# Decode block with backward pass: which arena slot a backward buffer gets, and where dependent side steps are cut

## The chip, the cores and the metric

The kernel runs on one core of one Trainium2 chip. The metric is device time in microseconds. A time is the median of several executions of the whole program; the profile is one further execution of it with the hardware profiler on.

## The reference

The kernel computes one decode step of a transformer block and all gradients of it. `A_` is attention over a cache, `B_` is a gated feed-forward layer:

```
x: 4 rows of 512;  k_cache, v_cache: 4 x 32 heads x 4096 x 128 (bf16)
q  = layernorm(x) @ wq                      # 32 heads of 128
p  = softmax(q k^T / sqrt(128));  o = p v
h  = x + o @ wo
h2 = h + (silu(ln(h) @ w1) * (ln(h) @ w3)) @ w2
out_0 = h2; out_1..out_8 = gradients of x, k_cache, v_cache, wq, wo, w1, w3, w2 for grad_out
```

The 128 pairs of batch and head have one query row each. The gradient of V for one head is the outer product of p and dO, the gradient of K the outer product of dS and q, with dS = p * (dO v^T - c) * scale. Both are as large as the caches, 1 MB a head, so the caches are read (V twice) and two arrays of the same size are written: 282 MB written and 423 MB read.

## The kernel before

**The arena.** Nearly all large buffers live in one tile, `arena`, of 23 slots of 4160 bf16 values in each partition, a little over 1 MB a slot. `Slot(name)` takes a slot and `give()` returns it; the order of the instructions is the order in which the code emits them, on each engine, and a slot may be given back as soon as its last use has been emitted: whoever takes it next waits by semaphore for that use to be over. `free` is a queue, so the slot given back first is taken first. `Slot2` takes two neighbouring slots for a buffer of 2 MB.

**Forward part.** For each of 128 heads, K and V are loaded, K is transposed, scores and softmax are computed for two heads at a time, and K scaled by p and V are multiplied to a small matrix. This part and the layer between (`mid`) are the same in both kernels.

**Backward part, single heads.** The first `SP` = 32 heads are worked one by one (steps `s`). In a step, V of head s + 5 is transposed on PE and evacuated by ACT (`front`, `V_T`, L790 and L791), `more_V` forms the V gradient 9 heads ahead of `s` (`grad_V`), `grad_K(s)` forms the K gradient; DVE writes each outer product into a slot (L796), and SP stores it (L807, L1234). From step 20 on (`part["B"]`), heads in preparation for the pairs below and side buffers share the arena: `part["pairs"]` names the 16 slots 0 to 5 and 8 to 17, eight pairs; the side buffers (`SIDE`) take the first slot of `free` that is not among them. Slot 7 holds small rows for the whole part.

**Backward part, pairs.** The other 96 heads go in 48 pairs (steps `t`). `load_pair` (L1259) loads V of two heads into a `Slot2`, `front_pair` transposes it (L1276 on PE, L1277 on ACT) three pairs ahead, `more_V` and `grad_pair` form the V gradient four pairs ahead and then the K gradient of pair t, both on DVE at L1357, stored by SP at L1367. POOL prepares the p column of each pair (L1354) and the dO window (L1268). `replicate_pair` writes replicated rows of q or dO (L1344 on PE, L1347 on ACT).

**Side work.** Everything else of the backward part, the gradients of x and of the weights, is in `side_work`, a generator. Each pair step runs two of its units before and two after its own gradients, a unit being what stands between two `yield`s. It computes dq (L1006 to L1011), puts it into the row buffer `flat` (POOL loads, L1015), transposes wq and forms dx (L1026 to L1047), stores dx (L1048), forms four pieces of the wq gradient in slots `gwq` (matmul L974, evacuation L968, store L1057), then loads w2 (L528), takes the row buffers `rows1` and `rows2`, loads grad_out into the first (`gr_bf`, L1066, on POOL), writes transposed rows into both (L1074 on PE, L1076 on ACT), forms the feed-forward output (`o_ps` on PE at L1086, the sum on DVE at L1091, stored at L1092) and the gradients of w2 (L1101), w1 and w3 (L1117) and wo (L1128).

Around `rows1` the code before reads:

```python
                nc.sync.dma_start(out=out_4[cc * P:(cc + 1) * P, :], in_=st.b(HD))
                st.give()
            flat.give()
            fs.give()
            w2 = load_w2()

            r1, r2 = Slot("rows1"), Slot("rows2")
```

At that moment `flat` and `fs` occupy slots 18 and 6, and the last `gwq` store is that of slot 22. The queue gives `w2` the slots 19 and 21, then `rows1` slot 22 and `rows2` slot 18.

Of the kernel before, what the change touches and what calls it, by code (L numbers as in the profile page):

```python
# [18 lines left out]
NSLOT = 23  # L19
JQ = 8  # L20
NPE = 1
SP = 32
NPAIR = 8


@with_exitstack
def kernel(
# [25 lines left out]
    B = A_x.shape[0]  # L53
# [9 lines left out]
    DC = D // P  # L63
# [43 lines left out]

    free = deque(range(NSLOT))
    part = {"B": False, "side_done": False}
    SIDE = ("Pp", "wq2", "dqflat", "fin", "rows1", "rows2", "oflat", "w2a", "w2b", "gwq", "gw2", "gw13", "gwo")  # L110
    arena = slotp.tile([P, NSLOT * SLOT], BF16, name="arena")

    class Slot:
        def __init__(self, name, src=free):
            if name in SIDE and part["B"]:
                self.i = next(i for i in free if i not in part["pairs"])
                free.remove(self.i)
            else:
                self.i = src.popleft()
            self.t = arena[:, self.i * SLOT:(self.i + 1) * SLOT]  # L120

        def b(self, n=4096):
# [6 lines left out]
            return self.t[:, 0:SJ * Dh].rearrange("p (j d) -> p j d", d=Dh)  # L129

        def give(self):
            free.append(self.i)

    class Slot2:
        @staticmethod
        def choices():
            at = {i: n for n, i in enumerate(free)}
            return [(max(at[i], at[i + 1]), i) for i in (range(0, NSLOT - 1, 2) if part["side_done"] else sorted(part["pairs"])[::2])
                    if i in at and i + 1 in at]

        def __init__(self):
            self.i = min(self.choices())[1]
# [2 lines left out]
            self.t = arena[:, self.i * SLOT:(self.i + 2) * SLOT]  # L145

        def give(self):
            free.append(self.i)
            free.append(self.i + 1)


    rows_t = pers.tile([32 + B, D], FP32, name="rows_t")
# [45 lines left out]
    for i in range(2):  # L198
        t = fcon.tile([P, 64], BF16, name=f"onesw{i}")
# [316 lines left out]
    def two_slots(nm):  # L516
        return [Slot(nm + "a"), Slot(nm + "b")]
# [7 lines left out]
    def load_w2():  # L525
        sl = two_slots("w2")
        for i in range(2):
            nc.sync.dma_start(out=sl[i].b(7 * D).rearrange("p (c j) -> p c j", c=7),  # L528
                              in_=B_w2.rearrange("(p c) j -> p c j", c=FC)[:, i * 7:(i + 1) * 7, :])
        return sl  # L530
# [247 lines left out]
    REP = B  # L778
    reps = {}
    V2s, VTs = {}, {}  # L780
# [34 lines left out]
    NV2 = 7  # L815
    vring = deque()
    nv = {"next": 0}
# [137 lines left out]
    with ExitStack() as c2:  # L955
# [44 lines left out]
        def side_work():  # L1000
# [4 lines left out]
            t = rs.f(2080)[:, 1536:1536 + NH]  # L1005
            nc.vector.tensor_tensor(out=t, in0=c_rep[:], in1=kPT[:], op=ALU.mult)  # L1006
            nc.vector.tensor_tensor(out=t, in0=dq_ps[:, 0:NH], in1=t, op=ALU.subtract)
            nc.vector.tensor_scalar(out=dqT_bf[:], in0=t, scalar1=scale, scalar2=None, op0=ALU.mult)
            pt = psg.tile([P, P], BF16, tag="gps", name="pt_dq")
            nc.tensor.transpose(pt[:], dqT_bf[:], ident_b[:])  # L1010
            nc.scalar.copy(out=dqr_bf[:], in_=pt[:])  # L1011
            flat = Slot("dqflat")
            yield
# [6 lines left out]
            for cc in range(DC):  # L1020
                wq2 = wq2s.popleft()
# [14 lines left out]
                load_wq2(cc + 2)  # L1036
                yield
            yield
            fs = Slot("fin")
            dxhat, lnbx, xh = (fs.f(3 * D)[0:B, k * D:(k + 1) * D] for k in range(3))  # L1040
            xhat_bf = fs.t[0:B, 6 * D:7 * D]
# [3 lines left out]
            layernorm_bwd_rows(lnbx, dxhat, xh, rstd_x[:], B)  # L1045
            dx_bf = rs.t[0:B, 3328:3328 + D]
            nc.vector.tensor_tensor(out=dx_bf, in0=dh, in1=lnbx, op=ALU.add)  # L1047
            nc.gpsimd.dma_start(out=o1_2, in_=dx_bf)  # L1048
            yield
            for cc in range(DC):  # L1050
                st = Slot("gwq")
                for n8 in range(HD // 512):
                    grad_unit(st.b(HD)[:, n8 * 512:(n8 + 1) * 512], xhat_bf[0:B, cc * P:(cc + 1) * P],
                              flat.b(HD)[0:B, n8 * 512:(n8 + 1) * 512])
                    yield
                grad_flush()
                nc.sync.dma_start(out=out_4[cc * P:(cc + 1) * P, :], in_=st.b(HD))  # L1057
                st.give()
            flat.give()
            fs.give()  # L1060
            w2 = load_w2()

            r1, r2 = Slot("rows1"), Slot("rows2")
            hh_rows, dg_rows, du_rows = r1.t[0:B, 0:F], r1.t[0:B, F:2 * F], r2.t[0:B, 0:F]
# [22 lines left out]
            for sl in w2:  # L1087
                sl.give()
            yield
            h2_bf = rs.t[0:B, 3328:3328 + D]  # L1090
            nc.vector.tensor_tensor(out=h2_bf, in0=hrows, in1=o2_ps[0:B, :], op=ALU.add)  # L1091
            nc.gpsimd.dma_start(out=o0_2, in_=h2_bf)  # L1092
            yield
            for i in range(2):
                st = Slot("gw2")
                hw = hh_rows[:, i * 7 * P:(i + 1) * 7 * P].rearrange("b (p k) -> b k p", k=7)
# [7 lines left out]
            oflat = Slot("oflat")  # L1104
# [49 lines left out]
        def replicate(nm_, i0):  # L1154
            if i0 >= NH or (nm_, i0 // REP) in reps:
                return
            K_ = 8 * B if i0 < 8 * B else P
            rows = dOrows_bf if nm_ == "rdo" else qrows_bf
            ps = psrep.tile([P, REP, Dh], FP32, tag="rep", name="rep_ps")
            for i in range(REP):  # L1160
                nc.tensor.matmul(ps[:, i, :], lhsT=ident_b[0:K_, i0 + i:i0 + i + 1].to_broadcast([K_, P]), rhs=rows[0:K_, :],
                                 start=True, stop=True)
            rt = rep_bufs[nm_][i0 // REP % 2]
            nc.scalar.copy(out=rt, in_=ps[:])
            reps[nm_, i0 // REP] = rt
# [28 lines left out]
        def front(s):  # L1194
            hl = s % B
            if s not in VTs:
                for g in range(SJ // GW):
                    V_T(s, psT, range(g, g + 1))
                    if hl == 0 and g == 0:
                        rows_out()  # L1200
                    if hl == 0 and g == 2:
                        rows_T()
            VT = VTs[s].heads()
            if hl == 0:
                rows["acc"] = psD.tile([P, 512], FP32, tag="dP", name="dP_ps")
            dO_window(s + 2)
            for u in range(2):
                for c in range(4):
                    j0 = 8 * c + 4 * u
                    nc.tensor.matmul(rows["acc"][32 * c:32 * (c + 1), :], lhsT=zq_window(zd[hl], 2 * hl + u),  # L1210
                                     rhs=VT[:, j0:j0 + 4, :], start=(hl == 0 and u == 0),
                                     stop=(hl == B - 1 and u == 1), tile_position=(0, 32 * c))
            if hl == B - 1:
                rows["ps"] = rows.pop("acc")
            sl = VTs.pop(s)
            (vring if nv["next"] < SP and len(V2s) + len(VTs) + len(vring) < NV2 else free).append(sl.i)

        def group_dS(g):
            i0 = g * B
# [22 lines left out]
        NT = (NH - SP) // 2  # L1242
        H0 = SP // B
        pV, pP2, pdS, psl = {}, {}, {}, {}
        npv = {"next": 0}
# [13 lines left out]
            nc.sync.dma_start(out=pV[t].t[:, 0:2 * SJ * Dh], in_=two_heads(A_v_cache, t))  # L1259

        def load_pairs(t):
            while npv["next"] < NT and (npv["next"] <= t or len(V2s) + 2 * len(pV) < 6 and len(Slot2.choices()) > 1):
                load_pair()

        def dO_pair(t):
# [44 lines left out]
        Pp, zt, P2b = {}, [], []  # L1310
# [23 lines left out]
        def replicate_pair(nm_, q):  # L1334
            if q >= NT // B or (nm_, "p", q) in reps:
                return
            s = SP + q * 2 * B
            K_ = 8 * B if s + 2 * B <= 8 * B else P
            rws = dOrows_bf if nm_ == "rdo" else qrows_bf
            ps = psrep.tile([P, REP, Dh], FP32, tag="rep", name="rep_ps")  # L1340
            for i in range(REP):
                for a in range(2):
                    n = s + i + a * B
                    nc.tensor.matmul(ps[64 * a:64 * (a + 1), i, :], lhsT=ident_b[0:K_, n:n + 1].to_broadcast([K_, P // 2]),  # L1344
                                     rhs=rws[0:K_, :], start=True, stop=True, tile_position=(0, 64 * a))
            rt = rep_bufs[nm_][(H0 + q) % 2]
            nc.scalar.copy(out=rt, in_=ps[:])  # L1347
            reps[nm_, "p", q] = rt
# [24 lines left out]
        def more_V(upto):  # L1373
            while gvd["n"] < min(SP, upto):
                s = gvd["n"]
                P_pairs(s)
                replicate("rdo", s - s % REP)
                grad_V(s)
                P_pairs(s + 1)
                P_pairs(s + 2)  # L1380
                gvd["n"] += 1
                if s % REP == 2 and s + 2 < SP:
                    replicate("rdo", s + 2)
                if s >= SP - 2:
                    P2_pair(s - SP + 2)
            while gvd["t"] < NT and SP + 2 * gvd["t"] + 2 <= upto:
                t = gvd["t"]
                P2_pair(t)
                replicate_pair("rdo", t // B)
                grad_pair(out_3, t, pP2.pop(t), reps["rdo", "p", t // B][:, t % B, :])  # L1390
                P2_pair(t + 1)
                gvd["t"] += 1
                if t % B == 2:
                    replicate_pair("rdo", t // B + 1)
# [57 lines left out]
        for t in range(NT):  # L1452
            s = SP + 2 * t
# [46 lines left out]
```

## Time and profile before

| | |
|---|---|
| median of 3 runs | 1698.37 us (1697.37 to 1699.48) |
| profiled execution | 1698.35 us, of which its span 1696.6 us |
| busy, share of the span | PE 73%, DVE 73%, ACT 57%, POOL 19% |
| DMA | 707.45 MB, mean 417 GB/s over the span |
| span in parts | forward and middle to about 740 us, single heads to about 960 us, pairs to the end |

A busy share is an average over the whole span; the slices of the page (40 of 42.4 us each) and the stretches of the trace show where it is high. A queue wait is read in three parts: the engine and line that waited, what ended the wait, and the sum, number and longest of the waits. "DMA out_dram<-arena" as the end of a wait means that a store had to land before its slot could be written again. The time from issue to landing of a DMA contains the time that it stood in the queue behind others.

### The profile page before, as it was taken

Reading aid. Unit: us, or ns where it says so; the run is one execution under the profiler, and the core shown is the slowest. Engines: PE = TensorE matmul, PEld = TensorE weight load, DVE = VectorE, ACT = ScalarE, POOL = GpSimd, SP = SyncE. Lnnn points to the kernel's source line nnn. Section 1 sums busy time; section 2 is a strip of 40 time slices with the busy share of each in tenths; the row PEclk is TensorE's granted clock in tenths of the full one; section 3 lists DMA queues with packets and bytes.
Section 4 is the critical chain, followed back from the end, with each engine's and each line's share of the span. In section 5 each row is a group of like instructions: output and inputs, shape, how many; then the busy total and the mean of one; then the engine's idle time right before and its main releaser. Section 6 shows DMA issues by size and latency. Waiting matters only on the chain. (4 is left out here: it accounts for less than half of the span.)

```text
span 1696.6 us, 37845 instructions
## 1 busy us (share of the span) xinstructions
PE 1245.9 (73%) x16228; PEld 953.4 (56%) x16228; DVE 1234.4 (73%) x1198; ACT 959.0 (57%) x1490; POOL 329.5 (19%) x583
## 2 busy tenths in 40 slices
PE   5889888888888888878877655666727767677552
PEld 4777766676677676756565544544425445445431
DVE  5989999999999987667764676575636665565582
ACT  3555444454455444677666566666628766566551
POOL 1211223222222222222331111021004110100000
PEclk9999999999999999798898689867659776666675
DMA  9999999999999999999999999999997999999998
GB/s 400 424 425 423 424 423 425 424 424 424 416 422 413 424 402 400 391 411 425 426 426 426 416 427 429 430 429 429 430 423 309 418 425 426 429 428 430 429 429 343
DMA packets 81000, 707.45 MB, mean 417 GB/s; under 512 B 8748, under 2 KB 12984, under 8 KB 15296
## 3 DMA queue, kind: packets, MB, share of 16 engines
q1 hardware_dynamic: 80416, 704.94, 99.0%
q8 instruction: 127, 2.08, 0.5%
q14 instruction: 41, 0.34, 0.0%
q0 software_dynamic: 416, 0.10, 0.0%
HBM read 422.59 MB, written 282.34 MB: 416 GB/s over the span
## 5 line engine op out<-in xcount | busy, mean ns | idle before, releaser
L1277 ACT COPY arena<-pt_tps 128x1024 bf16<-128x1024 bf16 x384 | 369.5, 1024 | 208.4 <-PE pt_tps L1276 208.0
L1276 PE MATMUL pt_tps<-ident_b,arena 128*128 128x128 bf16 x3072 | 309.7, 273 | 205.5 <-DMA arena<-in_A_v_cache_dram 124.1
L1276 PEld LDWEIGHTS <-arena 128*128 128x128 bf16 x3072 | 266.1, 126 | 307.2 <-issue 154.9
L1357 DVE TENSOR_TENSOR arena<-arena 128x8192 bf16<-128x8192 bf16 x48 | 212.3, 4424 | 255.6 <-DMA out_dram<-arena 223.7
L462 PE MATMUL M_ps<-arena 128*128 128x130 bf16 x4096 | 286.5, 222 | 37.8 <-DMA arena<-in_A_v_cache_dram 37.2
L447 DVE TENSOR_TENSOR arena<-arena 128x4096 bf16<-128x4096 bf16 x128 | 292.5, 2285 | 24.8 <-POOL arena L443 24.8
L462 PEld LDWEIGHTS <-arena 128*128 128x128 bf16 x4096 | 253.6, 99 | 58.7 <-DMA arena<-in_A_v_cache_dram 51.7
L354 DVE STREAM_TRANSPOSE arena<-arena 128x512 f32<-128x512 f32 (+1 forms) x321 | 250.6, 797 | 0.0
L349 ACT COPY arena<-pt_tps 128x1024 bf16<-128x1024 bf16 x128 | 129.4, 1012 | 186.7 <-PE pt_tps L348 151.7
L1357 DVE TENSOR_TENSOR arena<-dS,arena 128x8192 bf16<-128x8192 bf16 x48 | 212.4, 4427 | 19.6 <-DMA out_dram<-arena 19.4
L791 ACT COPY arena<-pt_tps 128x1024 bf16<-128x1024 bf16 x128 | 121.9, 1026 | 28.4 <-PE pt_tps L790 25.9
L360 POOL TENSOR_TENSOR W<-qrep,wmask 128x128 bf16<-128x128 bf16 x128 | 120.7, 943 | 85.4 <-PE S_ps L380 70.5
L1354 POOL COPY arena<-arena 128x128 bf16<-128x128 bf16 x48 | 38.8, 808 | 501.9 <-ACT arena L1331 276.3
L443 POOL COPY arena<-P_all 128x64 bf16<-128x64 bf16 x128 | 32.4, 253 | 413.6 <-ACT P_all L437 410.6
L790 PE MATMUL pt_tps<-ident_b,arena 128*128 128x128 bf16 x1024 | 82.1, 236 | 25.5 <-ACT arena L791 25.5
L1291 PE MATMUL dP_ps<-arena 128*32 128x512 bf16 x768 | 86.0, 484 | 7.8 <-ACT arena L1277 7.6
L790 PEld LDWEIGHTS <-arena 128*128 128x128 bf16 x1024 | 70.8, 108 | 36.1 <-issue 34.9
L437 ACT COPY P_all<-pt_P 32x64 bf16<-32x64 bf16 x256 | 51.9, 203 | 55.1 <-PE pt_P L433 52.9
L796 DVE TENSOR_TENSOR arena<-P,arena 128x4096 bf16<-128x4096 bf16 x29 | 66.3, 2296 | 20.1 <-DMA out_dram<-arena 19.7
L348 PE MATMUL pt_tps<-ident_b,arena 128*128 128x128 bf16 x1024 | 80.5, 223 | 0.0
L472 PE MATMUL kP_ps<-arena,onesw 128*32 128x512 bf16 x1024 | 79.2, 386 | 0.0
L796 DVE TENSOR_TENSOR arena<-dS,arena 128x4096 bf16<-128x4096 bf16 x32 | 73.5, 2302 | 6.6 <-DMA out_dram<-arena 6.2
(245 smaller groups left out, 1595.4 us busy)
## 6 DMA issues: line engine op xcount, KB each, us to landing
out_dram<-arena SPq DMA_DIRECT2D x96, 2048.0 KB, 27.7
arena<-in_A_v_cache_dram SPq DMA_DIRECT2D x160, 1024.0 KB, 15.8
arena<-in_A_k_cache_dram SPq DMA_DIRECT2D x128, 1024.0 KB, 15.4
arena<-in_A_v_cache_dram SPq DMA_DIRECT2D x48, 2048.0 KB, 31.7
out_dram<-arena SPq DMA_DIRECT2D x72, 1024.0 KB, 19.7
arena<-in_A_wq_dram SPq DMA_DIRECT2D x8, 1024.0 KB, 16.1
arena<-in_B_w_dram SPq DMA_DIRECT2D x8, 896.0 KB, 15.1
out_dram<-arena SPq DMA_DIRECT2D x6, 896.0 KB, 28.6
```

The lines of the kernel that those rows point to most:

```text
L349: nc.scalar.copy(out=KT[:, c * GW:(c + 1) * GW, :], in_=pt[:])
L354: nc.vector.transpose(out=KT[:, c * w_:(c + n) * w_], in_=Kn[:, c * w_:(c + n) * w_])
L360: nc.gpsimd.tensor_tensor(out=W[:, hl], in0=qrep[:, :, s:s + 1].to_broadcast([P, 4, 32]), in1=wmask[:, hl, None, :].to_broadcast([P, 4, 32 ...
L447: nc.vector.tensor_tensor(out=PK[:, :, 0:Dh].rearrange("p j (r t) -> p j r t", t=2), in0=Ks[s].heads().rearrange("p j (r t) -> p j r t", t=2),
L462: nc.tensor.matmul(hold["M"][:], lhsT=Vn[:, j, :], rhs=PK[:, j, :], start=(j == 0), stop=(j == SJ - 1))
L790: nc.tensor.transpose(pt[:, i, :], v[:, g * GW + i, :], ident_b[:])
L791: nc.scalar.copy(out=v[:, g * GW:(g + 1) * GW, :], in_=pt[:])
L796: nc.vector.tensor_tensor(out=dst.rearrange("p j (r t) -> p j r t", t=2), in0=col2[:, :, None, :].to_broadcast([P, SJ, Dh // 2, 2]), in1=r ...
L1276: nc.tensor.transpose(pt[:, i, :], v[:, g * GW + i, :], ident_b[:])
L1277: nc.scalar.copy(out=v[:, g * GW:(g + 1) * GW, :], in_=pt[:])
L1291: nc.tensor.matmul(rows["acc"][32 * c:32 * (c + 1), :], lhsT=zt[t % B][:, 32 - m:64 - m], rhs=v[:, j0:j0 + 4, :], start=(pl == 0 and u == ...
L1357: nc.vector.tensor_tensor(out=dst.rearrange("p (j r t) -> p j r t", r=Dh // 2, t=2), in0=col2[:, :, None, :].to_broadcast([P, 2 * SJ, Dh / ...
```

## The change

The change has four parts, all in the backward part.

1. Slots are chosen by an age, the number of slots stored since the slot was given back. A V slot that was only read is entered with an age of 4 more. From step 20 on a slot outside the pairs is taken by a side buffer, and by a gradient too if its age is at least `OLD` = 9; otherwise the oldest of all is taken. A `Slot2` is the pair whose younger half is oldest, whether it held a V pair or a gradient pair. `lnb`, a scratch buffer of dx, joins the side buffers.
2. `load_pairs` loads ahead only if the pair that it would take has an age of at least `OLD` - 2.
3. `flat` and `fs` are given back before the slot of the last `gwq` store, not after it.
4. Nine `yield`s are added to `side_work` and two removed, between steps that depend on each other, and `replicate_pair("rdo", 0)` is issued when the last single group has used its third head.

The diff, with the parts that only rename left out:

```diff
+OLD = 9
...
+    given = {"n": 0}
+
+    def age(i):
+        return given["n"] - given.get(i, -NSLOT)
+
+    def gave(*slots, stored=True):
+        given["n"] += len(slots) if stored else 0
+        for i in slots:
+            given[i] = given["n"] - (0 if stored else 4)
+            free.append(i)
...
-            if name in SIDE and part["B"]:
-                self.i = next(i for i in free if i not in part["pairs"])
-                free.remove(self.i)
-            else:
-                self.i = src.popleft()
+            self.i = src[0]
+            if part["B"] and src is free:
+                lone = sorted((i for i in free if i not in part["pairs"]), key=age, reverse=True)
+                self.i = lone[0] if name in SIDE or lone and age(lone[0]) >= OLD else max(free, key=age)
+            src.remove(self.i)
...
-            at = {i: n for n, i in enumerate(free)}
-            return [(max(at[i], at[i + 1]), i) for i in (range(0, NSLOT - 1, 2) if part["side_done"] else sorted(part["pairs"])[::2])
-                    if i in at and i + 1 in at]
+            return [(-min(age(i), age(i + 1)), i) for i in (range(0, NSLOT - 1, 2) if part["side_done"] else sorted(part["pairs"])[::2])
+                    if i in free and i + 1 in free]
...
             nc.vector.tensor_scalar(out=dqT_bf[:], in0=t, scalar1=scale, scalar2=None, op0=ALU.mult)
+            yield
+            yield
             pt = psg.tile([P, P], BF16, tag="gps", name="pt_dq")
             nc.tensor.transpose(pt[:], dqT_bf[:], ident_b[:])
+            yield
             nc.scalar.copy(out=dqr_bf[:], in_=pt[:])
...
             yield
+            yield
             fs = Slot("fin")
...
             nc.vector.tensor_tensor(out=dx_bf, in0=dh, in1=lnbx, op=ALU.add)
+            yield
+            yield
             nc.gpsimd.dma_start(out=o1_2, in_=dx_bf)
-            yield
...
                 nc.sync.dma_start(out=out_4[cc * P:(cc + 1) * P, :], in_=st.b(HD))
+                if cc == DC - 1:
+                    flat.give()
+                    fs.give()
                 st.give()
-            flat.give()
-            fs.give()
             w2 = load_w2()
+            yield
...
             for sl in w2:
                 sl.give()
             yield
+            yield
             h2_bf = rs.t[0:B, 3328:3328 + D]
             nc.vector.tensor_tensor(out=h2_bf, in0=hrows, in1=o2_ps[0:B, :], op=ALU.add)
+            yield
             nc.gpsimd.dma_start(out=o0_2, in_=h2_bf)
-            yield
...
-            (vring if nv["next"] < SP and len(V2s) + len(VTs) + len(vring) < NV2 else free).append(sl.i)
+            if nv["next"] < SP and len(V2s) + len(VTs) + len(vring) < NV2:
+                vring.append(sl.i)
+            else:
+                gave(sl.i, stored=False)
...
-            while npv["next"] < NT and (npv["next"] <= t or len(V2s) + 2 * len(pV) < 6 and len(Slot2.choices()) > 1):
+            while npv["next"] < NT and (npv["next"] <= t or len(V2s) + 2 * len(pV) < 6 and len(Slot2.choices()) > 1
+                                          and -min(Slot2.choices())[0] >= OLD - 2):
                 load_pair()
...
                 if s % REP == 2 and s + 2 < SP:
                     replicate("rdo", s + 2)
+                elif s % REP == 2:
+                    replicate_pair("rdo", 0)
```

More of the change, by code (lines that the diff above doesn't have):

```diff
@@ L109 @@
     part = {"B": False, "side_done": False}
-    SIDE = ("Pp", "wq2", "dqflat", "fin", "rows1", "rows2", "oflat", "w2a", "w2b", "gwq", "gw2", "gw13", "gwo")
+    SIDE = ("Pp", "lnb", "wq2", "dqflat", "fin", "rows1", "rows2", "oflat", "w2a", "w2b", "gwq", "gw2", "gw13", "gwo")
     arena = slotp.tile([P, NSLOT * SLOT], BF16, name="arena")
+    given = {"n": 0}
[6 more added lines that the diff above has]
+            free.append(i)
     class Slot:
         def __init__(self, name, src=free):
-            if name in SIDE and part["B"]:
-                self.i = next(i for i in free if i not in part["pairs"])
-                free.remove(self.i)
-            else:
-                self.i = src.popleft()
+            self.i = src[0]
[3 more added lines that the diff above has]
+            src.remove(self.i)
             self.t = arena[:, self.i * SLOT:(self.i + 1) * SLOT]
@@ L131, in give @@
         def give(self):
-            free.append(self.i)
+            gave(self.i)
     class Slot2:
@@ L147, in give @@
         def give(self):
-            free.append(self.i)
-            free.append(self.i + 1)
+            gave(self.i, self.i + 1)
     rows_t = pers.tile([32 + B, D], FP32, name="rows_t")
```

## The prediction

> **What bounds the kernel now.** I read three views in this order. First the page's slices: DMA is the resource that is full, all the way, except in two places.
>
> ```profile
> DMA  9999999999999999999999999999997999999998
> GB/s 400 424 425 423 424 423 425 424 424 424 416 422 413 424 402 400 391 411 425 426 426 426 416 427 429 430 429 429 430 423 309 418 425 426 429 428 430 429 429 343
> ...
> out_dram<-arena SPq DMA_DIRECT2D x96, 2048.0 KB, 27.7
> ...
> arena<-in_A_v_cache_dram SPq DMA_DIRECT2D x48, 2048.0 KB, 31.7
> ```
>
> No engine passes 73% busy. 707 MB at 430 GB/s would take 1645 us; the span is 1696.6 us. So the time is bytes over rate, and only a stretch in which the DMA queue runs dry can be won back. The slice with 309 GB/s (1272 to 1315 us) is such a stretch. The last slice is the drain of the last stores and stays. The two landing times say how deep the queue is: a store lands 27.7 us after its issue, and 27.7 us at 430 GB/s is 11.9 MB. An engine may therefore be late by almost that much before the queue is empty.
>
> Second, busy time and rate in stretches around the dip, and one earlier stretch (columns: stretch, PE, PEld, DVE, ACT and POOL busy, clock, DMA share, GB/s):
>
> ```profile
> 928.00:946.00 18.00, 12.13 (x128) 9.88 (x124) 16.67 (x12) 9.55 (x12) 3.94 (x3) 0.81 0.99 395
> 946.00:1190.00 244.00, 156.02 (x1635) 117.13 (x1636) 155.27 (x88) 152.12 (x180) 39.83 (x37) 0.78 1.01 429
> 1190.00:1250.00 60.00, 36.85 (x297) 25.10 (x297) 38.56 (x19) 31.49 (x41) 1.50 (x5) 0.59 1.01 430
> 1250.00:1262.00 12.00, 0.00 (x0) 0.00 (x0) 0.00 (x0) 0.00 (x0) 0.00 (x0) 0.50 1.00 425
> 1262.00:1276.00 14.00, 6.19 (x69) 4.11 (x69) 6.93 (x2) 6.98 (x9) 1.61 (x5) 0.62 0.92 389
> 1276.00:1300.00 24.00, 18.73 (x206) 12.15 (x203) 9.09 (x9) 18.58 (x23) 5.01 (x3) 0.93 0.62 253
> 1300.00:1320.00 20.00, 14.50 (x155) 10.46 (x153) 19.61 (x10) 17.59 (x23) 13.21 (x7) 0.84 1.01 390
> 1320.00:1440.00 120.00, 83.09 (x726) 56.17 (x724) 72.28 (x36) 80.54 (x106) 12.11 (x20) 0.70 1.01 425
> ```
>
> From 1250 to 1262 no engine executes anything, and the DMA lives on its backlog; the bill comes later. Third, who waited for whom between 1220 and 1320 us (total, times, longest):
>
> ```profile
> POOL arena L1066 <- DMA out_dram<-arena: 55.2, 1, 55.2
> ...
> PE pt_tps L1276 <- ACT arena L1277: 35.2, 16, 28.0
> ACT arena L1076 <- DMA out_dram<-arena: 28.9, 1, 28.9
> DVE arena L1357 <- POOL arena L1354: 19.9, 2, 19.6
> POOL arena L1354 <- ACT arena L1331: 18.4, 1, 18.4
> DVE arena L1091 <- PE o_ps L1086: 14.5, 1, 14.5
> ```
>
> One cause, in four steps. `rows1` takes slot 22, whose last wq-gradient store (L1057) was issued at 1238.07 us and lands 28.5 us later, with only the two w2 loads (1.8 MB) issued between that store and the reuse. The load of `gr_bf` (L1066) blocks POOL and the copy of `pt_Tr` (L1076) blocks ACT until 1267. Behind ACT stand the V evacuations (L1277), so PE stands still for 28.0 us; behind POOL stand the P pairs (L1354), so DVE waits 19.6 us. When PE comes back, `o_ps` is late and DVE, in order, waits 14.5 us at L1091 with the outer products behind it.
>
> **What the Trainium skill says.** "DMA: Bandwidth & Descriptors", section "Where 436 GB/s comes from", gives 435 GB/s as the ceiling of the 16 ports; the steady 429 to 430 agree, so there is no faster rate to hope for. The same page, "Anatomy of one DMA", says that DMA engines do not wait on semaphores, the issuing sequencer does. The trace agrees: at 1250 to 1262 everything issued goes on at 425 GB/s while every engine is blocked. "Perfetto Trace Analysis", "Optimization Strategy", says to find the gaps on the most-contended resource within its regime and follow the semaphore that ends them; the three views do this.
>
> **The change part by part.** I followed both allocators, and the order in which each program's DMAs are issued, and for each reuse of a slot counted the megabytes issued after the store that it must see landed. A reuse with more than about 12 MB behind its store waits for nothing; one with less waits for the difference, but leaves that much in the queue when it is released.
>
> (1) *Row buffers.* `flat` and `fs` are given back before the last gradient's slot, and side buffers take the unpaired slot that is longest without a store. `rows1` and `rows2` get slots 6 and 21 (those of `flat` and `fs`) instead of 22 and 18. These were read by PE alone: no store stands before L1066 or L1076. The four waits above go. Worth, against 430 GB/s: 14 x (1 - 389/430) = 1.3, 24 x (1 - 253/430) = 9.9, 20 x (1 - 390/430) = 1.9, together **13.1 us**. What is late next: the w2 loads, gw2 and gw13 slots now have 13 MB or more behind their stores; the outer products keep 10.5 to 11.5 MB as before, which costs DVE some 4.7 us of idle time a pair step (223.7 us over 48) and the DMA nothing.
>
> (2) *Slots by age and pairs like stored ones.* At the change from single heads to pairs, DVE waited in the window 895 to 946 us:
>
> ```profile
> DVE arena L1357 <- DMA out_dram<-arena: 15.5, 2, 14.2
> ...
> DVE arena L1357 <- ACT arena L1347: 11.9, 1, 11.9
> ```
>
> The 14.2 us is an outer product in slots 2 and 3, whose store had 5.2 MB behind it; in the new order that product goes into slots 14 and 15, with 11.5 MB behind. The lowest value left for DVE is 8.4, as before. The loss here is 18 x (1 - 395/430) = 1.5 us. Gain between 0 and 1.5; I take 1.0, as it is two waits out of three. Against it: the first V pair is loaded one step later (12.6 MB ahead of its use instead of 14.7), and one wq load on SP now waits for a store with 6.3 MB behind it. Behind that load stand a V pair and the stores; SP is released with 6.3/0.43 = 14.7 us of queue left, so I take 0, bounds 0 and 2 us.
>
> (3) *`replicate_pair("rdo", 0)` earlier*: the same instructions, 8 matmuls and one ACT copy of 0.58 us, moved ahead of the V transposes. This takes the 11.9 us wait above; it is inside the 1.5 us already counted, so 0 more.
>
> (4) *Separate units.* Net 7 more yields, at 4 units a pair step 1.75 steps of about 14.7 us (6.3 MB at 430 GB/s) later for all side work, its SP stores and loads and its four POOL row loads included. The last side store moves from pair step 40 to 41 of 48; six steps follow, so the end is the same. Waits such as PE on `dqT_bf` (8.6 us) and DVE at L1091 go, but under a full queue: 0 on their own. Bound: 0.5 us gain for an emptier neighbourhood, 1 us loss for a moved side store at the drain.
>
> (5) The stretch 1320 to 1440 runs at 425: 120 x (1 - 425/430) = 1.4 us. The part that is the queue refilling would go, the part that belongs to the side stores would stay; I take 0.3.
>
> Sum: 13.1 + 1.0 + 0.3 = 14.4 us off the profiled execution's 1698.35 us (span 1696.6 and 1.75 around it), which is the median of 1698.37 as good as exactly: **1684.0 us**. All together at their best, 16.0 us, give 1682.4, and the spread of the runs another 2 us down.
>
> **The rivals.**
> *A second cause inside the dip.* If the 14.5 us at L1091 had a reason of its own, the 9.9 us of the middle stretch would stay: 1698.4 - 1.3 - 1.9 - 1.0 = 1694. For it: the dip is deepest there. Against it: the w2 loads landed by 1270.8, while `o_ps` began at 1291.1, after PE's backlog of transposes; and two yields now separate it from L1091. Smaller leftovers of this sort (a third of the dip) give 1688.
> *The change doesn't do it.* If the rows still met a store, or the gap only moved to another reuse, the time stays at 1698. The slot numbers speak against it: no ACT or POOL wait with under 9 MB behind its store is left in the backward part.
> *Slower: the gate on pair loads.* `load_pairs` now asks for a pair of age 7 before it loads ahead. If V pairs fell back to being loaded only when due, each such step would miss 2.1 MB in the queue, a hole of 4.9 us. PE already waits 124 us in total for V. From four such steps on (19.6 us) the gain is more than eaten: 1684 + 19.6 = 1703.6. Against it: from pair step 4 on, each V load stands before the same stores as before, two steps ahead of its use.
>
> **How the numbers follow.** A measurement can tell about 0.2% (3.4 us) from no change here. Full recovery 0.70; a part of the dip stays, 1687 to 1694, 0.17; nothing happens 0.08; gate 0.05. Faster by over 0.2%: 0.70 + 0.17 and a little less for leftovers of nearly all, 0.87; within 0.08; slower 0.05. The range goes from 1680.5 (all gains and the runs' spread) to 1693 (most of the leftover cases), leaving out the last two cases and the worst leftovers.
>
> **What would show it.** In the profile after: the slice with 309 GB/s at 420 or more; no wait of ACT or POOL for `out_dram<-arena` on the lines of `pt_Tr` and `gr_bf`; no stretch without busy engines; PE's longest wait for ACT back to a few us; the 14.2 us of DVE gone. Step 2 is wrong if the rate around 930 us falls below 395; step 1 if the dip is still there with another name in front of DVE. A time above 1695 makes the prediction wrong.

## The result, and the profile after

The change makes no difference: 1698.49 us (1697.27 to 1699.24, 4 runs) against 1697.96 us for the kernel before (4 runs), ratio 1.0001, 95% interval 0.9984 to 1.0018. The profiled execution took 1698.19 us, its span is 1696.4 us, against 1698.35 and 1696.6. The prediction was 1684.0 us, at most 1693.0: it was wrong. Yet what it said of the dip came true. First the slices of the page and the landing time of the stores:

```profile
DMA  9999999999999999999999999999999999999995
GB/s 402 424 424 424 424 424 424 424 418 424 416 423 411 424 413 397 392 410 425 425 426 428 430 428 429 429 429 431 428 428 428 422 430 429 424 423 426 421 417 229
...
out_dram<-arena SPq DMA_DIRECT2D x96, 2048.0 KB, 27.8
```

The slice that had 309 GB/s has 428. But the last slice has 229 where it had 343. In bytes, 119 GB/s over a slice of 42.4 us are 5.0 MB more in the dip, and 114 GB/s are 4.8 MB less at the end: what was won in one slice is missing in the other. The same stretches as before (stretch, PE, PEld, DVE, ACT, POOL busy, clock, DMA share, GB/s):

```profile
928.00:946.00 18.00, 10.06 (x103) 8.00 (x102) 8.89 (x4) 8.72 (x11) 0.77 (x4) 0.81 1.01 430
1250.00:1262.00 12.00, 8.12 (x80) 5.09 (x78) 6.37 (x2) 8.34 (x11) 2.17 (x3) 0.78 1.01 429
1262.00:1276.00 14.00, 8.13 (x93) 6.39 (x95) 9.70 (x9) 9.42 (x11) 3.72 (x5) 0.76 1.01 427
1276.00:1300.00 24.00, 14.93 (x139) 10.82 (x133) 11.16 (x3) 11.08 (x14) 0.00 (x0) 0.78 1.01 430
1300.00:1320.00 20.00, 13.34 (x116) 10.17 (x117) 12.41 (x9) 11.31 (x14) 1.05 (x4) 0.67 1.01 425
```

None of these stretches is without busy engines, and no rate is below 425. Who waited for whom from 1220 to 1320 us (total, times, longest):

```profile
POOL arena L1376 <- DVE arena L1379: 49.1, 3, 27.5
DVE arena L1379 <- DMA out_dram<-arena: 43.0, 12, 12.4
...
PE pt_tps L1298 <- ACT arena L1299: 5.6, 15, 1.3
```

The waits of POOL and ACT for stores at `gr_bf` and `pt_Tr` are gone, PE waits for ACT 1.3 us at most where it was 28.0. What comes instead is at the end of the span:

```profile
1640.00:1664.00 24.00, 14.08 (x137) 11.13 (x136) 17.05 (x9) 14.11 (x17) 0.00 (x0) 0.70 1.00 427
1664.00:1668.00 4.00, 1.90 (x20) 0.74 (x16) 0.93 (x4) 1.48 (x2) 0.00 (x0) 1.00 0.50 213
1668.00:1674.00 6.00, 0.00 (x0) 0.00 (x0) 5.93 (x4) 0.00 (x0) 0.00 (x0) 0.51 0.06 25
1674.00:1684.00 10.00, 0.00 (x0) 0.00 (x0) 3.46 (x1) 0.00 (x0) 0.00 (x0) 0.50 0.99 421
1684.00:1694.00 10.00, 0.00 (x0) 0.00 (x0) 0.00 (x0) 0.00 (x0) 0.00 (x0) 0.50 0.06 26
```

In the kernel before, the last two of these stretches read:

```profile
1674.00:1684.00 10.00, 0.00 (x0) 0.00 (x0) 3.57 (x1) 0.00 (x0) 0.00 (x0) 0.50 1.01 433
1684.00:1694.00 10.00, 0.00 (x0) 0.00 (x0) 0.00 (x0) 0.00 (x0) 0.00 (x0) 0.50 0.39 167
```

The columns to read are the last two. A DMA share of 0.06 is 1/16: **one DMA engine of 16 works and fifteen stand still**. The last gradients have to wait for the last V load, and a load has landed only when the last of the 16 engines is done with its part: in both kernels this load ends, and PE goes on, at about 1656 us. The depth of the dip in the kernel before, a shorter stretch than those of the prediction, reads the same:

```profile
1291.00:1299.00 8.00, 6.74 (x65) 3.39 (x62) 4.69 (x2) 5.09 (x6) 3.73 (x2) 1.00 0.07 28
```

So the queue did not run dry there for all. It ran dry for fifteen engines, and one went on. The trace holds the time at which each engine reports its part of a transfer, 16 reports for each load and store. How far the last lies behind the ninth, in us, for transfers issued at about these times:

```
issued at    590   893   1058   1161   1254   1279   1312   1437   1619   1655
before       1.5   5.1    6.9    9.7   10.9   10.9    1.4    4.0    6.0    6.7
after        1.7   5.1    7.6   10.4   12.2   13.0   13.6   15.3   18.2   18.6
```

One engine falls behind (the added loads below find the same one at every step), by some 0.2 us with each store of 2 MB: its part of a store took 5.08 us, the others' 4.87 us, while on loads it keeps up. In the kernel before, the others wait for it in the dip, and the lag is nearly gone. After the change they don't wait there, the lag grows on to 18.6 us, and they wait for it at the end. The last reports themselves hardly differ between the kernels. In the kernel before they pass through the dip without a gap (1281.4, 1286.2, 1291.4, 1296.4, 1301.3, 1306.4 us), and those of the last two stores come at 1690.4 and 1695.3 us before, at 1690.3 and 1695.1 us after.

**Theory S**: this one engine is busy all the time in both kernels, and its work sets the time; an idle stretch of the others costs nothing. **Rival W**: the dip was a real loss of some 13 us, and other parts of the change gave the gain back later. A third view, called the mean rate in the expectations, is the one that the prediction used: bytes over the rate of all engines together.

### The profile page after: what moved, and what is told of

The parts are those of the page before. It is cut to its first block, busy times and chain, and to the rows that moved or that the text cites. A ratio compares the mean times of both kernels' runs of the same rounds, so it can differ in the third digit from the quotient of the medians.

```text
span 1696.4 us, 37844 instructions
## 1 busy us (share of the span) xinstructions
PE 1258.4 (74%) x16228; PEld 963.7 (57%) x16228; DVE 1235.0 (73%) x1198; ACT 960.8 (57%) x1490; POOL 336.7 (20%) x583
## 5 line engine op out<-in xcount | busy, mean ns | idle before, releaser
L1298 PE MATMUL pt_tps<-ident_b,arena 128*128 128x128 bf16 x3072 | 320.3, 279 | 202.6 <-DMA arena<-in_A_v_cache_dram 152.8
L1298 PEld LDWEIGHTS <-arena 128*128 128x128 bf16 x3072 | 275.6, 129 | 304.8 <-DMA arena<-in_A_v_cache_dram 179.5
L472 PEld LDWEIGHTS <-arena 128*128 128x128 bf16 x4096 | 255.9, 100 | 34.0 <-DMA arena<-in_A_v_cache_dram 23.7
L800 PE MATMUL pt_tps<-ident_b,arena 128*128 128x128 bf16 x1024 | 81.1, 234 | 26.3 <-ACT arena L801 26.3
L800 PEld LDWEIGHTS <-arena 128*128 128x128 bf16 x1024 | 69.6, 107 | 36.7 <-issue 35.4
L422 ACT ACTIVATE E<-S_ps,nm 128x256 f32<-128x256 f32 x64 | 30.4, 475 | 91.3 <-DVE nm L419 91.3
L358 PE MATMUL pt_tps<-ident_b,arena 128*128 128x128 bf16 x1024 | 80.6, 223 | 0.0
## 6 DMA issues: line engine op xcount, KB each, us to landing
arena<-in_B_w_dram SPq DMA_DIRECT2D x8, 896.0 KB, 14.9
```

The lines of the kernel that those rows point to most:

```text
L358: nc.tensor.transpose(pt[:, i, :], Kn[:, c * GW + i, :], ident_b[:])
L472: nc.tensor.matmul(hold["M"][:], lhsT=Vn[:, j, :], rhs=PK[:, j, :], start=(j == 0), stop=(j == SJ - 1))
L800: nc.tensor.transpose(pt[:, i, :], v[:, g * GW + i, :], ident_b[:])
L1298: nc.tensor.transpose(pt[:, i, :], v[:, g * GW + i, :], ident_b[:])
```

## The experiments

The runs came from three chips; each is compared with the kernel before on the same chip.

**The row buffers alone.** In the kernel before, `rows1` and `rows2` take the slots of `flat` and `fs` directly; nothing else of the change is there.

```diff
-            flat.give()
-            fs.give()
-            r1, r2 = Slot("rows1"), Slot("rows2")
+            r1, r2 = flat, fs
```

> The kernel before with one edit: rows1 and rows2 are the slots of flat and fs themselves, so nothing of the new slot ages, yields or pair loads is in it. Theory S (one of the 16 DMA engines is slower than the others, mostly in stores, and its own work sets the time; the dip at 1272 to 1315 us idled only the other fifteen): the dip goes, DMA share about 1.0 at 1290 us, but the time stays within 3 us of 1698, and the last 8 to 12 us before the end run at a DMA share of 0.06. Rival W (the dip was a real loss of 13 us, and the new order of slots, V loads and side units gave it back after 1340 us): 1685 us, with no long stretch at share 0.06 at the end.

Measured: 1698.19 us (12 runs) against 1698.64 (31 runs), ratio 0.9998 (0.9989 to 1.0007). Slices and two stretches:

```profile
GB/s 401 424 424 424 425 423 425 424 424 422 416 423 412 424 412 395 391 414 425 426 426 426 416 430 428 428 426 426 430 428 429 430 428 429 428 426 422 421 419 229
```
```profile
1670.00:1674.00 4.00, 0.00 (x0) 0.00 (x0) 4.00 (x2) 0.00 (x0) 0.00 (x0) 0.50 0.06 25
1684.00:1694.00 10.00, 0.00 (x0) 0.00 (x0) 0.00 (x0) 0.00 (x0) 0.00 (x0) 0.50 0.06 26
```

The dip is filled (429 instead of 309), the same 229 stands at the end, the lag ends at 17.6 us. W falls: with none of the other parts there, the 13 us still don't come.

**A stall put in.** In the changed kernel, one V evacuation on ACT is repeated, 28 times or (with 60 for 29) 59 times. PE stops at once, and DVE when it has no more prepared work.

```diff
-                nc.scalar.copy(out=v[:, g * GW:(g + 1) * GW, :], in_=pt[:])
+                for _ in range(29 if t == 33 and g == 0 else 1):
+                    nc.scalar.copy(out=v[:, g * GW:(g + 1) * GW, :], in_=pt[:])
```

> The changed kernel with the first V evacuation of pair 33 (emitted in pair step 30) repeated 28 times more on ACT, some 28 us in which ACT is not available, at a time when the fifteen faster DMA engines have about 10 us of work queued and the slow one 28 us. Theory S: a dip in the mean rate as in the kernel before, DMA share down to 0.06 for some us, and no more than 2 us in the time. If the mean rate set the time: 10 us slower, 1708.

> The changed kernel with the first V evacuation of pair 33 repeated 59 times more on ACT, some 59 us, where the run with 28 us cost about 2 us. Theory S: the slow DMA engine had about 28 us of work queued, so it runs dry too and the rest is lost: 20 to 32 us slower than the changed kernel, 1718 to 1730. If the time hung on the mean rate, the loss would start at the 10 us that the other fifteen had: 40 us and more.

Measured with 28 repeats, 28 x 1.022 = 28.6 us of ACT: 1700.94 us (20 runs) against 1698.64, ratio 1.0012 (1.0005 to 1.0019), 2.3 us more; S had allowed 2. The stretches around it:

```profile
1440.00:1460.00 20.00, 0.00 (x0) 0.00 (x0) 12.42 (x3) 19.39 (x20) 0.00 (x0) 0.50 1.00 428
1460.00:1470.00 10.00, 7.76 (x65) 5.44 (x65) 0.00 (x0) 8.26 (x10) 0.00 (x0) 0.57 0.75 320
1470.00:1480.00 10.00, 6.20 (x73) 4.10 (x69) 1.56 (x5) 7.95 (x12) 0.00 (x0) 0.94 0.07 29
1480.00:1490.00 10.00, 6.85 (x71) 4.11 (x69) 5.65 (x2) 8.16 (x12) 5.97 (x4) 0.84 0.49 169
```

A new dip, as deep as the old one (29 GB/s, share 0.07). By the rate of the stretches (110, 401 and 261 GB/s missing of 430, each over 10 us) it holds (1100 + 4010 + 2610)/430 = 18 us of lost rate, and it costs 2.3. The lag falls in it from 16.8 us (issued at 1458) to 2.4 us (1502). With 59 repeats: 1733.12 us (4 runs) against 1699.10, ratio 1.02 (1.0183 to 1.0217), 34.0 us more.

```profile
GB/s 401 424 424 424 424 423 424 424 422 424 419 424 407 423 415 395 379 424 425 426 426 428 430 427 429 430 428 428 432 428 422 422 429 374 7 386 426 426 427 365
```

Now a slice has 7 GB/s, less than a sixteenth of 430: the slow engine too had nothing to do. 31 more repeats are 31.7 us of ACT and cost 34.0 - 2.3 = 31.7 us more. So a stall was free up to what the slow engine had in its queue, some 26 us here, and had its full price above. That is the edge that S asks for, but the total lies between the two expectations: 1733.12 is above the 1718 to 1730 of S, and 34.0 us is below the 40 of the mean rate.

**Which engine it is.** The Trainium skill, "DMA: Bandwidth & Descriptors", section "Why a DMA increments its semaphore by 16 and not by 1", says that a transfer is spread over the largest number k up to 16 that divides the slowest dimension on both sides, and that for transfers such as SP's these are the lowest-numbered engines. The trace agrees as far as it goes: a transfer of k = 1 to 14 rows left k + 1 reports. Which engines they were it doesn't show, so the numbers of engines below rest on the page. So transfers of 1 to 16 rows of 16 bytes, one in each of 16 pair steps, sound out which engine is late:

```diff
+            if 20 <= t < 36:
+                k = t - 19
+                nc.sync.dma_start(out=rs.t[0:k, 4032 + 8 * (k - 1):4032 + 8 * k], in_=A_v_cache[0, 0, 0:k, 0:8])
```

> The changed kernel with one tiny extra load in each of the pair steps 20 to 35, of k = 1 to 16 partitions by 16 bytes. By the Trainium skill (same section as before) such a load uses the k lowest DMA engines. Theory S: a probe that includes the slow engine lands some 10 to 18 us later than one that does not, so the smallest k with a late landing names the engine. If instead all engines are late by turns, the landings vary with k without a step. Time: within 3 us of 1698 in either case.

Measured: one run, 1698.75 us. With one to four rows the last report came 9.0 to 13.3 us after the issue; with five rows 29.9 us, and with any more 27 to 28. The fifth-lowest engine, number 4, is the slow one, from k = 5 on in every step. (The page's section "Latency and other measured facts" names engines 7 and 15 as usually slower; here it was neither.)

**Less work for the slow engine, by cut loads.** Six runs cut V pair loads by partitions. The edit is the same in all but for the line of the cuts; in the kernel before it stands at L1259:

```diff
-            nc.sync.dma_start(out=pV[t].t[:, 0:2 * SJ * Dh], in_=two_heads(A_v_cache, t))
+            cuts = (0, 120, P) if t in (4, 14, 24, 34, 44) else (0, P)
+            for r0, r1 in zip(cuts, cuts[1:]):
+                nc.sync.dma_start(out=pV[t].t[r0:r1, 0:2 * SJ * Dh], in_=two_heads(A_v_cache, t)[r0:r1])
```

These cuts of 120 + 8, in the changed kernel and in the one before:

> The changed kernel with five of the 48 V pair loads (t = 4, 14, 24, 34, 44) cut in a DMA of 120 partitions and one of 8. By the Trainium skill (DMA: Bandwidth & Descriptors, Why a DMA increments its semaphore by 16) a load of 120 partitions runs on the 15 lowest engines and one of 8 partitions on the 8 lowest, so the 16th engine is left out of five loads, 4.9 us of work each. Theory S, if the slow engine is that 16th one: it is relieved of up to 24 us, the other fifteen decide, which were through at 1684 with a 5 us hole in which they waited for the last V load: 1680 to 1686 us. Theory S, if the slow engine is another one: 1698 to 1703. Rival W: 1698, the loads are the same bytes.

> The kernel before with the same five V pair loads cut in 120 and 8 partitions. Theory S with the 16th engine as the slow one: it is no longer behind when the dip comes, so the dip idles all sixteen and now costs; the lag of about 6.7 us that is left at the end goes: 1690 to 1695 us, so 8 to 12 us slower than the changed kernel with the same cut. Rival W: 1698, or no difference between the two kernels with the cut.

One load cut 124 + 4, in the changed kernel and (with t == 20) in the one before:

```diff
+            cuts = (0, 124, P) if t == 34 else (0, P)
```

> The changed kernel with one of the 48 V pair loads (t = 34) cut in DMAs of 124 and 4 partitions. 124 and 4 have 4 as their largest divisor up to 16, so by the Trainium skill (same section) both run on the 4 lowest DMA engines; the probes put the slow engine just above them, at the fifth place. Theory S: the slow engine has 8 x 0.61 = 4.9 us less to do, the first four 24 x 0.61 = 14.6 us more, which they have free by then (they land about 20 us before it): 4 to 5 us faster than the changed kernel, 1693 to 1695. If the slow engine does not set the time, or the loads cost what bytes cost: 1698 or slower.

> The kernel before with V pair load t = 20, issued about 40 us ahead of its stall, cut in the same way. Theory S: the slow engine has 4.9 us less queued when the stall comes, so it runs dry earlier inside the dip and wins little or nothing: 1697 to 1700 us, 3 us or more above the changed kernel with its cut load. That the cut helps as much here as there (1694) would speak against the part of S that says the dip is free only because of the slow engine's backlog.

Seven loads in five pieces, in the changed kernel, the pieces of four or of five rows:

```diff
+            cuts = (0, 112, 116, 120, 124, P) if t in range(20, 48, 4) else (0, P)
```
```diff
+            cuts = (0, 112, 117, 122, 127, P) if t in range(20, 48, 4) else (0, P)
```

> The changed kernel, but seven of the 2 MB V pair loads (t = 20, 24, ..., 44) are issued in five pieces of 112, 4, 4, 4 and 4 partitions. By the completion counts of the earlier runs a load of 112 partitions uses all 16 DMA engines with 7 rows each, and one of 4 partitions uses the four lowest engines with one row each. Against an uncut load each of the engines 0 to 3 gets 11 rows instead of 8 and the engine with number 4 gets 7; a row takes 0.61 us (4.87 us per 8 rows in the trace). Theory S (the engine with number 4 sets the time, the others have some 18 us in hand at the end): it is relieved of 7 rows, 4.3 us, and the four lowest get 21 rows, 12.8 us more, which stays within what they have in hand: 1694 us (1692.5 to 1697, the upper end for what 28 more transfers cost by themselves). Mean-rate view (bytes over a common rate): no gain, 1698.5 us, or some 1 to 8 us more if small pieces cost by themselves; the same as the twin with pieces of 5.

> As its twin with pieces of 4, the same seven loads in the same number of pieces and the same bytes, but of 112, 5, 5, 5 and 1 partitions: a piece of 5 uses the five lowest engines, so the engine with number 4 gets 10 rows instead of 8, and engines 0 to 3 get 10 or 11. Theory S: the engine with number 4 has 14 rows, 8.5 us, more to move, and the time goes up by as much: 1707 us (1705 to 1710), 12.8 us above the twin. Mean-rate view: the same as the twin within 1.5 us, since neither bytes nor pieces differ.

```
                         us        ratio to before (95%)        wanted by S
120 + 8, after       1725.80    1.0156 (1.0141 to 1.0171)       1680 to 1686, or 1698 to 1703 (other engine): both missed
120 + 8, before      1719.66    1.0121 (1.0099 to 1.0143)       1690 to 1695: missed; 8 to 12 above its twin: 6.1 below
124 + 4, after       1705.54    1.0040 (1.0027 to 1.0052)       1693 to 1695: missed
124 + 4, before      1708.81    1.0058 (1.0044 to 1.0072)       1697 to 1700: missed; 3 or more above its twin: 3.3
112 + 4 x 4, after   1710.46    1.0071 (1.0059 to 1.0084)       1692.5 to 1697: missed
112 + 3 x 5 + 1      1720.55    1.0129 (1.0113 to 1.0144)       1705 to 1710: missed; 12.8 above its twin: 10.1
```

None brought a gain. The traces say part of why. The pieces of 120 + 8 rest on a wrong assumption: they take one of the sixteen engines out of the large piece, but not number 4, which got a row more. The 124 rows went over four engines with 31 rows each and landed 42 us after their issue; at the end two engines are 18 to 19 us behind the ninth report, can be followed back to that load, and set the time. And in all of them more rows were slow around the cuts. 16 KB rows that took over 1 us between 880 and 1680 us: 82 in the changed kernel, 569 with 120 + 8, 308 and 419 in the two with five pieces. In the last run the last reports of the gradient stores fall back 5.8 us at the first cut and 5.4 us at the second against the changed kernel, of which the two rows more account for 1.2 us each time. Besides, the five pieces hold up SP. Its transfers use eight completion semaphores in turn, and each waits for the one that it will use. So around the first cut of four-row pieces SP issued only at the moment at which the eighth transfer before had landed (issued at 1189.5 and 1215.4 us, the eighth before landed at 1189.5 and 1215.3). With four small pieces among eight transfers, the other engines had too little to do:

```profile
1200.00:1210.00 10.00, 4.35 (x33) 3.45 (x34) 0.70 (x2) 4.13 (x5) 0.00 (x0) 0.50 0.63 202
```

These six runs therefore can't be read as a relief of the slow engine alone. Only the sign within the last pair, 10.1 us for one engine's rows at equal bytes and pieces, spoke for S.

**More work for the slow engine, without a cut.** The clean form leaves all loads and stores as they are, and adds to the changed kernel 18 transfers of four, or of five, rows of 16 KB from DRAM to DRAM:

```diff
+    scr = nc.dram_tensor("scr_dram", [18, 5, 8256], BF16).ap()
...
+            if 20 <= t < 38:
+                nc.sync.dma_start(out=scr[t - 20, 0:4, 0:8192], in_=A_v_cache[0, 0:4, 0:64].rearrange("h t d -> h (t d)"))
```

> The changed kernel with 18 additional transfers on SP's queue, one at the end of each pair step t = 20 to 37: four rows of 16 KB, from the input V to scratch space in DRAM that nothing reads. No load or store of the kernel is cut, no buffer of SBUF is touched. By the counts of the earlier runs such a transfer gives one row to each of the four lowest DMA engines and nothing to the one with number 4. If a row takes 0.61 us as the other 16 KB rows do, engines 0 to 3 get 11.0 us more work. Theory S (the engine with number 4 alone sets the time; the others have 18 us in hand at the end): nothing, 1698.5 us (1697.5 to 1700), the lag of the last completions behind the median as before. Mean-rate view (bytes over the common rate): 18 x 64 KB read and written again, 1.2 MB at 427 GB/s, 2.8 us: 1701.3; or more if any transfer in the queue costs the others time.

> As its twin with four rows, but each of the 18 transfers has five rows, so that the engine with number 4 gets one row of each as well. Theory S: that engine has 18 rows of 0.61 us, 11.0 us, more to move, and the time goes up by as much: 1709.5 us (1707 to 1713), 11 us above the twin; the last completion of each load and store falls behind by 0.6 us more per step. Mean-rate view: 1.5 MB, 3.5 us: 1702.0, 0.7 us above the twin.

Measured with four rows: 1697.75 us (13 runs), ratio 0.9998 (0.9990 to 1.0006). With five rows: 1711.09 us (5 runs), ratio 1.0077 (1.0064 to 1.0091). **Four engines are given 18 rows each and nothing happens; a fifth is given its 18 rows and the time rises by 13.3 us.** In the trace the four rows have landed 8.9 to 14.9 us after their issue, while the fifth comes after 26 to 30 us, 0.61 to 0.68 us behind the last report of the load or store ahead of it. A long stretch and the end of both spans, four rows first, then five:

```profile
1440.00:1660.00 220.00, 141.00 (x1205) 97.71 (x1202) 137.67 (x64) 133.42 (x170) 20.41 (x23) 0.68 1.01 428
1670.00:1673.00 3.00, 0.00 (x0) 0.00 (x0) 3.00 (x2) 0.00 (x0) 0.00 (x0) 0.50 0.06 27
1684.00:1693.00 9.00, 0.00 (x0) 0.00 (x0) 0.00 (x0) 0.00 (x0) 0.00 (x0) 0.50 0.06 25
```
```profile
1440.00:1660.00 220.00, 145.63 (x1209) 101.74 (x1209) 132.22 (x58) 133.94 (x172) 18.63 (x23) 0.66 1.00 410
1698.00:1708.00 10.00, 0.00 (x0) 0.00 (x0) 0.00 (x0) 0.00 (x0) 0.00 (x0) 0.50 0.06 25
```

With five rows the last report of the last store comes at 1708.1 us, with four at 1694.7: 13.4 us, the whole difference in the time. From 1440 to 1660 us the mean rate is 410 and not 428: the others are held back to the slow engine's pace. Of the 13.3 us, the 18 rows themselves are 11.6 (18 times 0.61 to 0.68); where the rest comes from was not followed up. There were more slow rows here too, without any cut: 169 over 1 us, where the run with four rows had 46.

## Why the prediction was wrong

**The step that failed** is the first one: "So the time is bytes over rate, and only a stretch in which the DMA queue runs dry can be won back". 430 GB/s is the sum over 16 engines, and the sum is not what ends last. A queue can run dry for fifteen engines and not for the sixteenth, and then there is nothing to win. The clue was in the view that the prediction used, one question further: the stretch 1276 to 1300 showed a share of 0.62, but its depth, 1291 to 1299, shows 0.07.

**The queue's depth** was sized wrongly by the same cause. "A store lands 27.7 us after its issue, and 27.7 us at 430 GB/s is 11.9 MB" holds for the last engine only. At about 1270 us the ninth report came some 11 us before the last, so the others had that much less in hand.

**Step 1, the row buffers, 13.1 us.** The mechanism was right to the line: slots, waits, the dip. Its worth is 0, as the run with the row buffers alone shows (0.45 us faster, and the interval of the ratio includes 1).

**Step 2, slots by age, 1.0 us.** The rate from 928 to 946 us rose from 395 to 430. In the stretch 895 to 946 the 14.2 us of DVE are gone:

```profile
DVE arena L1379 <- DMA out_dram<-arena: 15.0, 3, 7.9
```

Its worth is 0 too: the whole kernel is no faster. That this filled stretch was free for the same reason was not tried by itself.

**Steps 3 and 4, both at 0**: nothing in the result speaks against them. **Step 5, 0.3 us**: the rate from 1320 to 1440 went from 425 to 426, and the time did not follow.

**"The last slice is the drain of the last stores and stays"** was wrong, and it is where the gain went: 343 became 229 GB/s.

**The rivals.** "The change doesn't do it" gave the right time, 1698, at 8 in 100, but for another reason: it looked for a gap at another reuse of a slot, and there is none; the others' waiting moved to the end of the span. The gate on pair loads did no harm that can be seen in the time: the waits of PE for V in the pairs grew from 124.1 to 152.8 us in total, the longest from 8.1 down to 7.3. A second cause inside the dip had no part in it.

**What would show it.** All five signs in the profile came true around the dip (of DVE's waits for stores in the pairs the longest left is 12.4 us). They were signs of the mechanism, and none of its worth. A sign of worth would have been the last report of the stores ahead of the end, or the share in the depth of the dip.

What stays open: why this engine needs longer for stores. In the last stores of the changed kernel, when it works alone, each of its rows takes 0.611 us like those of the others; in one store just before, with the others at work, its rows took 0.611 to 0.634 us. That it is slowed by the others' work is possible, and was not tried. Open too: whether its work can be taken off it without the price that the cut loads had. No run here is faster than the kernel before.

## What to carry to other kernels

When the DMA queues are full, ask which of the 16 engines ends last, not what their mean rate is: compare the last report of a transfer with the middle one, along the whole span. In the depth of a dip read the DMA share; 1/16 means that one engine still works, and if that engine also ends last, as here, filling the dip brings nothing. A cheap proof is a pair of added transfers that differ by one engine.

## What the runs showed of the hardware

- DMA engine number 4 was slower on the stores of this kernel: 5.08 us against 4.87 us for its part of 2 MB, and it set the time in both kernels. Two chips, one with the added loads of 1 to 16 rows and one with the added copies of four and five, gave the same number.
- Of a stall of ACT, PE and DVE some 26 us were free: 28.6 us cost 2.3 us.
- Most 16 KB rows took 0.611 us. Around V loads cut by partitions more of them took over 1 us (569 against 82 with five loads cut 120 + 8), and these five cost 27 us together; which resource they met at was not settled.
